# Pooling k and v of two batches with a band matrix on TensorE in place of additions on GpSimd

## The chip, the cores and the metric

The kernel runs on one core of a Trainium2 chip. A core has TensorE (PE in the profile, its weight loads PEld), VectorE (DVE), ScalarE (ACT), GpSimd (POOL) and SyncE (SP), which here issues all DMAs from one queue in order. Each engine works off its own list of instructions in order and waits on semaphores for the others. The metric is the device time of one execution in microseconds; lower is better.

## The reference

Three parts follow each other. Attention with pooled keys and values, for 4 batches, 8 heads, 576 tokens and a head size of 64; a first expert layer of 512 to 2048 to 512 with h * cos(h); and eight gated experts of 512 to 1024 to 512, whose gates are normalised over rows and columns eight times. The part that the change touches:

```python
    pool = 8
    Sp = S // pool                                          # 72 pooled rows
    k_p = k.reshape(B, H, Sp, pool, D).mean(axis=3)
    v_p = v.reshape(B, H, Sp, pool, D).mean(axis=3)
    scores = scale * np.matmul(q, k_p.transpose(0, 1, 3, 2))
    scores = scores - np.max(scores, axis=-1, keepdims=True)
    attn = np.exp(scores)
    attn = attn / (np.sum(attn, axis=-1, keepdims=True) + 1e-09)
    return np.matmul(attn, v_p).astype(np.float32)
```

The weights of the first expert layer come as float64 and are turned into float32 in the kernel. Products of the expert layers are made of three products of rounded parts (a high part and a remainder on each side).

## The kernel before

**Tiles and stages.** The 2304 tokens are 6 blocks of 384, each of three chunks of 128. A batch has 576 tokens, so block 0 needs batch one alone, block 1 batches one and two, block 2 batch two, block 3 batch three, block 4 batches three and four, block 5 batch four. The stages overlap. In the head, attention of block 0 is computed and the first unit of the expert weights is converted; then the loop over tasks (unit u of weights and block j) runs hidden products, the nonlinearity and output products, and between them takes attention of later blocks from one list (`attn_queue`) and conversions of later weights from another (`conv_queue`). The gated experts follow from about 400 us on.

**Attention.** `attn_weights` asks for the pooled keys of the batches of its block, calls `load_k` for those not there yet, loads q, makes the scores (`scores`, L277, tile psc; a product of a q chunk with `kbd`, the pooled keys of a pair of heads on a diagonal of blocks), subtracts the maximum on VectorE (L334, L335), takes the exponential on ScalarE (L336) and normalises (`normalize`: sum at L338, multiplication at L297). `attn_values` calls `load_v` where needed, transposes the probabilities on TensorE (L353, tile ptr) and multiplies them by the pooled v (L360, tile px); ScalarE and VectorE split the result into two parts (L367, L368).

**Pooling.** Batch one has its own functions. Its k is added up on VectorE and its v by TensorE: v lies in rows of tokens, 128 tokens to a tile, and is multiplied by `band`, a matrix of ones and zeros of 136 columns, of which the 72 columns from an offset select, for a tile of tokens, the pooled row that each token belongs to (`pool_first_v`, L248, five products of 512 columns). For batches two to four `load_k` and `load_v` fetch four tiles each, one per pair of heads, already laid out with the 8 members of a pool as the middle dimension (tiles kr, vr), and `pool_sum` (L200, L202) adds them in three steps of halves on GpSimd; then `fill_kbd` copies the pooled keys into one of two `kbd` tiles on ScalarE (L207). The tiles kr and vr come from the pool of buffers `rawp`, which has three buffers of one tag. The same three serve the units of weights that `load_unit` reads back (L102).

**Conversions.** `convert` turns a piece of float64 weights into float32 with one operation on ScalarE (L116), five on VectorE (L117 to L125) and one on GpSimd (L126), and writes it to memory (L127). `split` makes the two parts of weights: ScalarE the high one (L94), VectorE or GpSimd the remainder (L95).

**What sets the order.** The code records operations in program order, and a scheduler puts each engine's list in an order of its own, by dependences and by its model of times. So a change of one operation moves others on all engines.

Of the kernel before, what the change touches and what calls it, by code (L numbers as in the profile page):

```python
# [10 lines left out]
F32 = mybir.dt.float32  # L11
# [7 lines left out]
B, H, S, D = 4, 8, 576, 64  # L19
POOL = 8  # L20
SP = S // POOL
HP = H // 2
P = 128
T = B * S
DM = H * D
# [12 lines left out]
SINKHORN_ITERS = 8  # L38
EPS = 1e-9
G2 = 32  # L40
BAND0 = S // POOL // 16 * 16


# [12 lines left out]


@with_exitstack
def fused_kernel(ctx: ExitStack, tc: tile.TileContext, qT, kT, vT, v0, wa1, wb1, wa2, wb2, wg, out):
    nc = tc.nc  # L60

    const = ctx.enter_context(tc.tile_pool(name="const", bufs=1))
# [2 lines left out]
    rawp = ctx.enter_context(tc.tile_pool(name="rawp", bufs=3))  # L65
# [4 lines left out]
    ps_a = ctx.enter_context(tc.tile_pool(name="ps_a", bufs=2, space=bass.MemoryType.PSUM))  # L70
# [97 lines left out]
    def right(stack, name, bufs, **more):  # L168
        return stack.enter_context(tc.tile_pool(name=name, bufs=bufs, side="right", **more))
# [3 lines left out]
    kp = right(early, "kp", 2)  # L173
# [22 lines left out]
    def pool_sum(out, r, engine):  # L196

        n = POOL // 2
        while n > 1:
            engine.tensor_tensor(out=r[:, :n], in0=r[:, :n], in1=r[:, n:2 * n], op=ALU.add)  # L200
            n //= 2
        engine.tensor_tensor(out=out, in0=r[:, 0], in1=r[:, 1], op=ALU.add)  # L202

    def fill_kbd(b, ks):
        kbd = kbds[b % 2]
        for j in range(2):
            nc.scalar.activation(out=kbd[j * D:(j + 1) * D, :, j * SP:(j + 1) * SP],  # L207
                                 in_=ks[j * D:(j + 1) * D], func=AF.Copy)
        kpool[b] = kbd
# [11 lines left out]
    def load_first_v():  # L221

        tiles = []
        for tag in ("xl2", "xh3", "xl5"):
            t = xp.tile([P, 2, DM], F32, tag=tag, name="v0")
            for i in range(2):
                o = len(tiles) * P
                rows = min(P, S - o)
                if rows > 0:
                    nc.sync.dma_start(out=t[:rows, i, :], in_=v0[o:o + rows, :])  # L230
                    tiles.append((t[:rows, i, :], rows))
        return tiles

# [6 lines left out]
                                     in_=ks[j * D:(j + 1) * D], func=AF.Copy)  # L240
        kpool[0] = kbds[0]

    def pool_first_v(tiles):

        pv = ps_a.tile([SP, DM], F32, tag="pa", name="pv")
        for c, (t, rows) in enumerate(tiles):
            o = BAND0 - c * P // POOL
            nc.tensor.matmul(out=pv, lhsT=band[:rows, o:o + SP], rhs=t, start=(c == 0), stop=(c == len(tiles) - 1))  # L248
        vs = kp.tile([SP, H, D], F32, tag="vs", name="vs")
        nc.scalar.activation(out=vs.rearrange("p h d -> p (h d)"), in_=pv, func=AF.Copy)  # L250
        vpool[0] = vs

    def load_k(b):
        ks = kp.tile([P, HP, SP], F32, tag="ks", name="ks", bufs=1)
        for hp in range(HP):
            kr = rawp.tile([P, POOL, SP], F32, tag="raw", name="kr")
            nc.sync.dma_start(out=kr, in_=kT[:, b, hp])
            pool_sum(ks[:, hp], kr, nc.gpsimd)
        fill_kbd(b, ks)

    def load_v(b):
        vs = kp.tile([SP, H, D], F32, tag="vs", name="vs")
        for hp in range(HP):
            vr = rawp.tile([SP, POOL, 2 * D], F32, tag="raw", name="vr")
            nc.sync.dma_start(out=vr, in_=vT[:, b - 1, hp])
            pool_sum(vs[:, 2 * hp:2 * hp + 2, :].rearrange("p h d -> p (h d)"), vr, nc.gpsimd)
        vpool[b] = vs

# [38 lines left out]
    def attn_first(qcs, g):  # L307

        at = at_tile(0, g)
        for i in range(TPB):  # L310
            ps = scores(i, g, qcs[i][:, 2 * g:2 * g + 2], (ps_s, "ps") if i % 2 == 0 else (ps_a, "pa"))
            mx = sp.tile([P, 4, 1], F32, tag="mx", name="mx")
            nc.vector.tensor_reduce(out=mx.rearrange("p h o -> p (h o)"), in_=ps, op=ALU.max, axis=AX.X,
                                    negate=True)
            nc.vector.tensor_scalar(out=mx, in0=mx, scalar1=SCALE, scalar2=None, op0=ALU.mult)
            sm = sp.tile([P, 4, 1], F32, tag="sm0", name="sm0")
            for h in range(4):
                nc.scalar.activation(out=at[:, i, h, :], in_=ps[:, h, :], func=AF.Exp, scale=SCALE,
                                     bias=mx[:, h, :], accum_out=sm[:, h, :])
            normalize(at[:, i], sm)  # L320
# [140 lines left out]
    for what in 'kqfqqvfff':  # L461
        if what == "k":
            kr0 = load_first_k()
        if what == "q":
            qcs.append(load_q(len(qcs)))
        if what == "v":
            vr0 = load_first_v()
        if what == "f":
            raws.append(load_piece(0, len(raws)))
    pool_first_k(kr0)  # L470
    vpool[0] = None
    for g in range(2):
        attn_first(qcs, g)
        if g == 0:
            pool_first_v(vr0)
    for g in range(2):
        attn_values(0, g)

# [2 lines left out]
    def open_gate():  # L481
# [13 lines left out]
        nc.scalar.activation(out=wg2[:, :, :E], in_=wgr, func=AF.Copy)  # L495
        nc.vector.tensor_tensor(out=wg2[:, :, G2:G2 + E], in0=wgr, in1=wg2[:, :, :E].bitcast(F32), op=ALU.subtract)
        sel = gc.tile([G2 + E, E], F32, name="sel")
        nc.vector.tensor_tensor(out=sel, in0=ident[:G2 + E, :E], in1=ident[:G2 + E, G2:G2 + E], op=ALU.add)
        gate.update(ones=ones, wg2=wg2, sel=sel, lg=gc.tile([P, NT, E], F32, name="lg"),
                    pr=gc.tile([P, NT, E], F32, name="pr"))  # L500

    def logits(j):
# [389 lines left out]
```

## Time and profile before

| | us |
|---|---|
| median of 3 runs | 2053.98 (2053.37 to 2056.27) |
| the profiled execution, its own time | 2056.55 |
| span of its instructions | 2054.7 |
| PE busy in the span | 2008.2 (98%) |
| DVE busy | 1254.5 (61%) |
| ACT busy | 899.3 (44%) |
| POOL busy | 818.1 (40%) |

The slices of the page show where the engines are busy. The first slices are the head:

```profile
PE   6799999999999999999999999999999999999999
DVE  8987785655685555555666555555565655555553
ACT  6675566656533334333444343343343343333431
POOL 7755653433333234243443342342353432433420
PEclk8899999999999999999999999999999999999999
```

A slice is 51 us long, and a digit is the busy share in tenths (9 is 90% or more). Busy time of PE is modelled and holds overlaps; the granted clock stands as a share of 2.4 GHz, so 0.75 in a stretch is half of it at 2.4 and half at 1.2 GHz. An operation's time on DVE or POOL holds what it waits for inside the engine once it has begun.

### The profile page before, as it was taken

To read this page: it belongs to the slowest core of one execution; us is meant where nothing else is said; L and a number is where in the kernel's file an instruction comes from. 1 tells how busy PE (TensorE), PEld (TensorE's weight loads), DVE (VectorE), ACT (ScalarE), POOL (GpSimd) and SP (SyncE) were. 2 spreads that over 40 slices of the span, in tenths; PEclk is the share of its full clock that TensorE was granted. 3 is DMA by queue.
4 is the path that set the end of the run, shared out by engine and by line. 5 is a ranking of instruction groups with operands and counts; after the bars stand their busy time and mean duration, and the time that the engine had idled before them with its cause. 6 is when DMAs were issued, how large, how long until landed. Compare 5 with 4: busy or idle time off the path is not lost.

```text
span 2054.7 us, 27450 instructions
## 1 busy us (share of the span) xinstructions
PE 2008.2 (98%) x10339; PEld 1817.8 (88%) x10339; DVE 1254.5 (61%) x2003; ACT 899.3 (44%) x1781; POOL 818.1 (40%) x646
## 2 busy tenths in 40 slices
PE   6799999999999999999999999999999999999999
PEld 5689899999888889989888888888898888898887
DVE  8987785655685555555666555555565655555553
ACT  6675566656533334333444343343343343333431
POOL 7755653433333234243443342342353432433420
PEclk8899999999999999999999999999999999999999
DMA  7433331211311212212232122121132221221210
GB/s 257 140 126 124 110 121 47 83 52 62 123 63 62 68 56 82 62 62 74 70 123 72 52 83 72 52 82 62 62 107 92 69 72 54 80 72 52 83 42 31
DMA packets 53636, 167.46 MB, mean 81 GB/s; under 512 B 6112, under 2 KB 9952, under 8 KB 53504
## 3 DMA queue, kind: packets, MB, share of 16 engines
q1 hardware_dynamic: 53504, 165.72, 24.9%
q8 instruction: 81, 1.33, 0.3%
q14 instruction: 51, 0.42, 0.1%
HBM read 149.44 MB, written 16.25 MB: 81 GB/s over the span
## 4 chain that ended last, share of the span: by engine, by line
PE 88%; DVE 5%; DMA 1%; ACT 1%; issue 1%; POOL 1%; SPq 0%; DVEq 0%; ACTq 0%; POOLq 0%
PE po L135 15%; PE po L136 15%; PE po L137 15%; PE py L683 14%; PE pv L683 10%; PE px L683 10%; PE ph L136 2%; PE ph L135 2%; PE ph L137 2%; DVE m L121 1%; DVE at L297 1%; DVE cw L125 0%; DMA wb1f<-cw 0%; DVE m L119 0%; DVE r L387 0%
## 5 line engine op out<-in xcount | busy, mean ns | idle before, releaser
L95 POOL TENSOR_TENSOR wlo<-raw,whi 128x512 fp32r<-128x512 f32 x248 | 345.2, 1410 | 680.9 <-ACT gh L671 489.6
L135 PE MATMUL po<-whi,gh 128*128 128x512 f32 x1152 | 455.1, 395 | 0.6 <-DVE acc L733 0.6
L136 PE MATMUL po<-wlo,gh 128*128 128x512 f32 x1152 | 454.4, 394 | 0.0
L137 PE MATMUL po<-whi,gl 128*128 128x512 f32 x1152 | 454.0, 394 | 0.0
L94 ACT ACTIVATE whi<-raw 128x512 fp32r<-128x512 f32 x488 | 290.3, 625 | 220.6 <-PE py L683 184.8
L739 DVE SCALAR_TENSOR_TENSOR acc<-po,pr,acc 128x512 f32<-128x512 f32 x252 | 188.7, 749 | 292.4 <-PE po L137 288.2
L683 PE MATMUL py<-xc,whi 128*128 128x384 f32 x1152 | 293.7, 335 | 0.0
L95 DVE TENSOR_TENSOR wlo<-raw,whi 128x512 fp32r<-128x512 f32 x240 | 216.7, 903 | 125.6 <-ACT whi L94 60.5
L137 PEld LDWEIGHTS po<-whi,gl 128*128 128x128 f32 x1152 | 216.2, 188 | 50.1
L135 PEld LDWEIGHTS po<-whi,gh 128*128 128x128 f32 x1152 | 216.1, 188 | 42.3 <-DVE acc L733 0.8
L136 PEld LDWEIGHTS po<-wlo,gh 128*128 128x128 f32 x1152 | 215.7, 187 | 37.9
L683 PEld LDWEIGHTS py<-xc,whi 128*128 128x128 f32 x1152 | 210.1, 188 | 12.3
L683 PE MATMUL py<-xc,wlo 128*128 128x384 f32 x576 | 192.7, 335 | 0.0
L587 POOL TENSOR_TENSOR s<-raw 128x512 f32<-128x512 f32 x48 | 63.2, 1317 | 312.1 <-DMA raw<-wa 288.9
L683 PE MATMUL pv<-xc,whi 128*128 128x384 f32 x640 | 169.4, 338 | 2.0 <-DVE gl L672 2.0
L671 ACT ACTIVATE gh<-c 128x384 fp32r<-128x384 f32 x96 | 50.2, 523 | 224.2 <-DVE c L711 224.2
L135 PE MATMUL ph<-xh,whi 128*128 128x384 f32 x384 | 130.3, 343 | 5.1 <-DVE r L387 5.0
L683 PE MATMUL px<-xc,whi 128*128 128x384 f32 x512 | 134.8, 335 | 0.0
L136 PE MATMUL ph<-xl,whi 128*128 128x384 f32 x384 | 130.6, 341 | 0.7 <-DVE xl L368 0.7
L136 PE MATMUL po<-gl,whi 128*128 128x384 f32 x384 | 129.2, 337 | 0.6 <-POOL gl L390 0.6
L137 PE MATMUL ph<-xh,wlo 128*128 128x384 f32 x384 | 129.2, 337 | 0.0
L137 PE MATMUL po<-gh,wlo 128*128 128x384 f32 x384 | 128.3, 337 | 0.0
(161 smaller groups left out, 3635.9 us busy)
## 6 DMA issues: line engine op xcount, KB each, us to landing
raw<-wa SPq DMA_DIRECT2D x112, 512.0 KB, 4.5
raw<-wb SPq DMA_DIRECT2D x112, 512.0 KB, 3.6
raw<-wa1f SPq DMA_DIRECT2D x14, 512.0 KB, 3.7
raw<-wb1f SPq DMA_DIRECT2D x14, 512.0 KB, 3.7
out<-acc SPq DMA_DIRECT2D x18, 256.0 KB, 4.3
wa1f<-cw SPq DMA_DIRECT2D x16, 256.0 KB, 2.9
wb1f<-cw SPq DMA_DIRECT2D x16, 256.0 KB, 2.8
qc<-qt SPq DMA_DIRECT2D x30, 128.0 KB, 4.2
```

The lines of the kernel that those rows point to most:

```text
L94: nc.scalar.activation(out=hi, in_=src, func=AF.Copy)
L95: lo_engine.tensor_tensor(out=lo, in0=src, in1=hi.bitcast(F32), op=ALU.subtract)
L121: v.scalar_tensor_tensor(out=m, in0=high, scalar=-2**30, in1=m, op0=ALU.bitwise_and, op1=ALU.bitwise_or)
L135: nc.tensor.matmul(out=ps, lhsT=lh, rhs=rh, start=(i == 0), stop=False)
L136: nc.tensor.matmul(out=ps, lhsT=lh, rhs=rl, start=False, stop=False)
L137: nc.tensor.matmul(out=ps, lhsT=ll, rhs=rh, start=False, stop=(i == n - 1))
L297: engine.tensor_tensor(out=at[:, r], in0=at[:, r], in1=rs[:, r].to_broadcast([P, 4, SP]), op=ALU.mult)
L587: nc.gpsimd.tensor_tensor(out=out, in0=x, in1=y, op=op)
L671: nc.scalar.activation(out=gh, in_=c, func=AF.Relu)
L683: marks["pe"] = nc.tensor.matmul(out=ps, lhsT=l[:, k], rhs=r[:, c, :], start=(start and c + n == 0), stop=(last and n == 2), skip_group_ch ...
L739: nc.vector.scalar_tensor_tensor(out=a, in0=po, scalar=pe, in1=a, op0=ALU.mult, op1=ALU.add)
```

## The change

For batches two and three (`BANDED`) k and v come as rows of tokens, 128 to a tile, and are pooled by products with `band` on TensorE. `load_rows` fetches a batch's 576 rows in five DMAs into three tiles of `rawp`. `load_k` makes twenty products, four pairs of heads by five tiles of tokens, with the rows as weights and 72 columns of `band` moving, into one PSUM tile (pk) of the pool `ps_a`, from which `fill_kbd` copies. `load_v` does for these batches what was done for batch one alone: five products of 512 columns with `band` as weights, and a copy by ScalarE. Batch one's k is still added up on VectorE, and batch four's k and v on GpSimd. The host lays the tensors out to suit.

```diff
+BANDED = range(1, B - 1)
...
-    def pool_first_v(tiles):
+    def pool_v(b, tiles):
...
         pv = ps_a.tile([SP, DM], F32, tag="pa", name="pv")
         for c, (t, rows) in enumerate(tiles):
             o = BAND0 - c * P // POOL
             nc.tensor.matmul(out=pv, lhsT=band[:rows, o:o + SP], rhs=t, start=(c == 0), stop=(c == len(tiles) - 1))
         vs = kp.tile([SP, H, D], F32, tag="vs", name="vs")
         nc.scalar.activation(out=vs.rearrange("p h d -> p (h d)"), in_=pv, func=AF.Copy)
-        vpool[0] = vs
+        vpool[b] = vs
+
+    def load_rows(src):
+
+        tiles = []
+        for i in range(0, S, 2 * P):
+            raw = rawp.tile([P, 2, DM], F32, tag="raw", name="rows")
+            for c in range(2):
+                o = i + c * P
+                rows = min(P, S - o)
+                if rows > 0:
+                    nc.sync.dma_start(out=raw[:rows, c, :], in_=src[o:o + rows, :])
+                    tiles.append((raw[:rows, c, :], rows))
+        return tiles
 
     def load_k(b):
-        ks = kp.tile([P, HP, SP], F32, tag="ks", name="ks", bufs=1)
-        for hp in range(HP):
-            kr = rawp.tile([P, POOL, SP], F32, tag="raw", name="kr")
-            nc.sync.dma_start(out=kr, in_=kT[:, b, hp])
-            pool_sum(ks[:, hp], kr, nc.gpsimd)
+        if b in BANDED:
+
+            tiles = load_rows(kn[b - 1])
+            ks = ps_a.tile([P, HP, SP], F32, tag="pa", name="pk")
+            for hp in range(HP):
+                for c, (t, rows) in enumerate(tiles):
+                    o = BAND0 - c * P // POOL
+                    nc.tensor.matmul(out=ks[:, hp, :], lhsT=t[:, hp * P:(hp + 1) * P], rhs=band[:rows, o:o + SP],
+                                     start=(c == 0), stop=(c == len(tiles) - 1))
+        else:
+            ...
         fill_kbd(b, ks)
 
     def load_v(b):
+        if b in BANDED:
+            pool_v(b, load_rows(vn[b]))
+            return
```

The scheduler's lists change with it. Lines of the changed kernel stand 2 lower in its first part and 28 lower from the scores on (L305 is the old L277, L381 the old L353, L388 the old L360).

On PE, at the first block's values and the first hidden products (kbd_126 holds the keys of batch one, kbd_128 those of batch two, ph is a hidden product, px a product with v), the list before reads:

```order
L353 MATMUL ptr<-ident,at 72x128 x4
L137 MATMUL ph<-xh_278,wlo 128x384
L135 MATMUL ph<-xh_278,whi 128x384
L136 MATMUL ph<-xl_279,whi 128x384
L137 MATMUL ph<-xh_278,wlo 128x384
L360 MATMUL px<-pt,vs 64x384 x4
L277 MATMUL psc<-kbd_128,qc 64x144
L277 MATMUL psc<-kbd_126,qc 64x144
L277 MATMUL psc<-kbd_128,qc 64x144
L277 MATMUL psc<-kbd_128,qc 128x144 x2
L135 MATMUL ph<-xh_278,whi 128x384 x2
```

The list after, from the same values on:

```order
L388 MATMUL px<-pt,vs 64x384 x4
L137 MATMUL ph<-xh_278,whi 128x384 x2
L276 MATMUL pk<-band,rows 128x72 x20
L138 MATMUL ph<-xl_279,whi 128x384
L139 MATMUL ph<-xh_278,wlo 128x384
```

And, ten hidden products behind pk:

```order
L305 MATMUL psc<-kbd_128,qc 64x144
L305 MATMUL psc<-kbd_126,qc 64x144
L305 MATMUL psc<-kbd_128,qc 64x144
L305 MATMUL psc<-kbd_128,qc 128x144 x2
L250 MATMUL pv<-rows,band 72x512 x5
L305 MATMUL psc<-kbd_126,qc 128x144 x2
```

The twenty products of pk stand two hidden products behind px, where the scores with batch two's keys stood; twelve hidden products are now ahead of those scores, and the five products of pv of batch two stand between them and the next block's first scores.

On POOL, behind the first block's normalisation (cw and wlo are a conversion and a remainder of weights), the list before reads:

```order
L202 TENSOR_TENSOR ks<-kr 128x72
L200 TENSOR_TENSOR vr<-vr 72x512
L126 TENSOR_TENSOR cw<-m,cw 128x512
L200 TENSOR_TENSOR vr<-vr 72x512
L126 TENSOR_TENSOR cw<-m,cw 128x512
L200 TENSOR_TENSOR vr<-vr 72x256
L200 TENSOR_TENSOR vr<-vr 72x512
L95 TENSOR_TENSOR wlo<-cw,whi 128x512
L200 TENSOR_TENSOR vr<-vr 72x256
L202 TENSOR_TENSOR vs<-vr 72x128
```

The list after, at the same two conversions:

```order
L97 TENSOR_TENSOR wlo<-cw,whi 128x512
L128 TENSOR_TENSOR cw<-m,cw 128x512 x2
L97 TENSOR_TENSOR wlo<-cw,whi 128x512 x2
L128 TENSOR_TENSOR cw<-m,cw 128x512
L97 TENSOR_TENSOR wlo<-cw,whi 128x512
L128 TENSOR_TENSOR cw<-m,cw 128x512
L418 TENSOR_TENSOR gl<-r,gh 128x384
```

The additions of kr, ks, vr and vs are gone from between them; conversions and remainders follow one another.

On SP, at v of batch three and k of batch four (qc is q, raw_1631 and the like float64 weights), the list before reads:

```order
L265 DMA vr<-vt 72x1024
L331 DMA qc<-qt 128x256
L434 DMA raw_1417<-wb 128x1024
L331 DMA qc<-qt 128x256
L127 DMA wa1f<-cw 128x512
L257 DMA kr<-kt 128x576 x2
L434 DMA raw_1452<-wb 128x1024
L257 DMA kr<-kt 128x576
L331 DMA qc<-qt 128x256
L127 DMA wa1f<-cw 128x512
L257 DMA kr<-kt 128x576
```

The list after:

```order
L264 DMA rows<-vn 128x512
L129 DMA wa1f<-cw 128x512
L264 DMA rows<-vn 128x512 x3
L264 DMA rows<-vn 64x512
L359 DMA qc<-qt 128x256 x2
L462 DMA raw_1631<-wb 128x1024
L129 DMA wa1f<-cw 128x512
L359 DMA qc<-qt 128x256 x2
L282 DMA kr<-kt 128x576 x3
L359 DMA qc<-qt 128x256
L282 DMA kr<-kt 128x576
```

The last four DMAs of vr became five of rows; the first three of kr now follow one another, and the weights and the write that stood among them stand ahead of them or behind. On PE the scores that need these keys (kbd_128 again) stand, behind the five products of pv of batch three, after 33 hidden and output products, seven score products and twelve transposes.

## Rows read from the trace of the kernel before

**Rows 1.** Busy time by stage: window, length, engines busy (instructions), clock, DMA.
```profile
20.00:46.00 26.00, 18.20 (x92) 12.93 (x93) 24.50 (x43) 17.18 (x40) 23.59 (x27) 0.77 0.67 212
46.00:98.00 52.00, 40.59 (x220) 33.45 (x220) 51.36 (x81) 31.05 (x54) 41.70 (x44) 0.85 0.54 161
98.00:140.00 42.00, 40.17 (x242) 34.72 (x242) 38.09 (x78) 29.62 (x52) 21.16 (x22) 1.00 0.41 127
...
240.00:280.00 40.00, 34.30 (x201) 31.80 (x200) 35.07 (x57) 21.74 (x45) 26.54 (x25) 1.00 0.43 134
```

**Rows 2.** Waits of PE, 20 to 98 us: total us, times, longest.
```profile
PE psc L277 <- DVE at L335: 5.9, 2, 5.7
```

**Rows 3.** DVE groups by shape, 20 to 98 us: busy us, mean ns, idle before.
```profile
L297 DVE TENSOR_TENSOR at<-at,rs 128x288 f32<-128x288 f32 x12 | 14.0, 1220 | 0.0
L121 DVE SCALAR_TENSOR_TENSOR m<-raw,m 128x512 int32<-128x512 int32 x9 | 9.2, 1031 | 0.0
L119 DVE TENSOR_SCALAR m<-m 128x512 int32<-128x512 int32 x8 | 7.2, 910 | 0.0
...
L117 DVE TENSOR_SCALAR m<-m 128x512 f32<-128x512 f32 x8 | 6.8, 859 | 0.1
...
L124 DVE TENSOR_SCALAR cw<-m 128x512 int32<-128x512 int32 x8 | 5.8, 741 | 0.0
```

**Rows 4.** The same operations, whole span: duration min/median/max in ns.
```profile
L117 DVE TENSOR_SCALAR m<-m x32: 410/462/2117, 9.5 to 302.8; 128x512 f32<-128x512 f32 x32
L119 DVE TENSOR_SCALAR m<-m x32: 357/428/2321, 9.9 to 304.7; 128x512 int32<-128x512 int32 x32
L121 DVE SCALAR_TENSOR_TENSOR m<-raw,m x32: 674/694/4725, 10.4 to 306.4; 128x512 int32<-128x512 int32 x32
L124 DVE TENSOR_SCALAR cw<-m x32: 410/428/1711, 11.5 to 307.4; 128x512 int32<-128x512 int32 x32
L297 DVE TENSOR_TENSOR at<-at,rs x30: 444/458/2923, 47.7 to 316.9; 128x288 f32<-128x288 f32 x30
```

**Rows 5.** Stage 20 to 98 us: L200, then L202; DVE and POOL busy.
```profile
20.00:98.00 78.00, 0.00 (x0) 29.74 (x32) 0.82 0.59 178
...
20.00:98.00 78.00, 0.00 (x0) 9.13 (x16) 0.82 0.59 178
```

**Rows 6.** Timeline of PEld at 14 us: start, us, operation, idle before.
```profile
14.35 0.14 PEld L248 LDWEIGHTS pv<-v,band 128*72 128x72 f32 x1 [0.29 <-issue]
14.78 0.14 PEld L248 LDWEIGHTS pv<-v,band 128*72 128x72 f32 x1 [0.29 <-issue]
```

**Rows 7.** Timeline of PE at 404 us, a small product's six records.
```profile
404.54 0.83 PE L514 MATMUL pq<-sel,lt 40*128 40x8 f32 x6
405.30 0.44 PE L508 MATMUL pl<-xh,wg 128*128 128x384 f32 x1
```

**Rows 8.** Timeline of PE at 101 us, at full clock.
```profile
101.14 0.33 PE L136 MATMUL po<-gl,whi 128*128 128x384 f32 x1
101.31 0.34 PE L137 MATMUL po<-gh,wlo 128*128 128x384 f32 x1
101.49 0.65 PE L277 MATMUL psc<-kbd,qc 128*128 128x144 f32 x4
101.98 0.27 PE L353 MATMUL ptr<-ident,at 128*72 128x128 f32 x1
```

**Rows 9.** Timeline of PE at 43 us, behind the long wait.
```profile
43.69 1.30 PE L277 MATMUL psc<-kbd,qc 128*128 128x144 f32 x4 [5.67 <-DVE at L335]
```

**Rows 10.** The copy of pooled v from PSUM by ACT, batch one.
```profile
L250 ACT ACTIVATE vs<-pv x1: 593/593/593, 18.2 to 18.2; 72x512 f32<-72x512 f32 x1
```

**Rows 11.** The tiles kr: durations in ns, first and last start, DMA landing.
```profile
L200 POOL TENSOR_TENSOR kr<-kr x24: 482/794/1361, 16.3 to 113.7; 128x288 f32<-128x288 f32 x12, 128x144 f32<-128x144 f32 x12
L257 SPq DMA_DIRECT2D kr<-kt x12: 328/355/423, 10.0 to 106.6; - x12
L202 POOL TENSOR_TENSOR ks<-kr x12: 325/514/850, 22.4 to 116.1; 128x72 f32<-128x72 f32 x12
...
DMA to landing us min/median/max: 2.9/3.7/4.5
```

**Rows 12.** Timeline of SP at 92 us, the fourth batch's first k tiles.
```profile
92.54 1.98 SPq L257 DMA_DIRECT2D kr<-kt  x2
```

More of the change, by code (lines that the diff above doesn't have):

```diff
@@ L58, in fused_kernel @@
 @with_exitstack
-def fused_kernel(ctx: ExitStack, tc: tile.TileContext, qT, kT, vT, v0, wa1, wb1, wa2, wb2, wg, out):
+def fused_kernel(ctx: ExitStack, tc: tile.TileContext, qT, kT, kn, vT, vn, wa1, wb1, wa2, wb2, wg, out):
     nc = tc.nc
@@ L229, in load_first_v @@
                 if rows > 0:
-                    nc.sync.dma_start(out=t[:rows, i, :], in_=v0[o:o + rows, :])
+                    nc.sync.dma_start(out=t[:rows, i, :], in_=vn[0, o:o + rows, :])
                     tiles.append((t[:rows, i, :], rows))
@@ L250, in pool_first_v @@
         nc.scalar.activation(out=vs.rearrange("p h d -> p (h d)"), in_=pv, func=AF.Copy)
-        vpool[0] = vs
-    def load_k(b):
-        ks = kp.tile([P, HP, SP], F32, tag="ks", name="ks", bufs=1)
-        for hp in range(HP):
-            kr = rawp.tile([P, POOL, SP], F32, tag="raw", name="kr")
-            nc.sync.dma_start(out=kr, in_=kT[:, b, hp])
-            pool_sum(ks[:, hp], kr, nc.gpsimd)
+        vpool[b] = vs
[10 more added lines that the diff above has]
+        return tiles
+    def load_k(b):
+        if b in BANDED:
[7 more added lines that the diff above has]
+        else:
+            ks = kp.tile([P, HP, SP], F32, tag="ks", name="ks", bufs=1)
+            for hp in range(HP):
+                kr = rawp.tile([P, POOL, SP], F32, tag="raw", name="kr")
+                nc.sync.dma_start(out=kr, in_=kT[:, 1, hp])
+                pool_sum(ks[:, hp], kr, nc.gpsimd)
         fill_kbd(b, ks)
     def load_v(b):
+        if b in BANDED:
+            pool_v(b, load_rows(vn[b]))
+            return
         vs = kp.tile([SP, H, D], F32, tag="vs", name="vs")
@@ L264, in load_v @@
             vr = rawp.tile([SP, POOL, 2 * D], F32, tag="raw", name="vr")
-            nc.sync.dma_start(out=vr, in_=vT[:, b - 1, hp])
+            nc.sync.dma_start(out=vr, in_=vT[:, hp])
             pool_sum(vs[:, 2 * hp:2 * hp + 2, :].rearrange("p h d -> p (h d)"), vr, nc.gpsimd)
@@ L474, in fused_kernel @@
         if g == 0:
-            pool_first_v(vr0)
+            pool_v(0, vr0)
     for g in range(2):
@@ L854, with rows @@
     qt = q.reshape(B, HP, 2, S, D).transpose(2, 4, 1, 0, 3).reshape(P, HP, NT, P).transpose(0, 2, 1, 3)
-    kt = k.reshape(B, HP, 2, SP, POOL, D).transpose(2, 5, 0, 1, 4, 3).reshape(P, B, HP, POOL, SP)
-    vt = v[1:].reshape(B - 1, HP, 2, SP, POOL, D).transpose(3, 0, 1, 4, 2, 5).reshape(SP, B - 1, HP, POOL, 2 * D)
-    v0 = v[0].transpose(1, 0, 2).reshape(S, DM)
+    def rows(a):
+        return a.transpose(0, 2, 1, 3).reshape(-1, S, DM)
+    kt = k[::B - 1].reshape(2, HP, 2, SP, POOL, D).transpose(2, 5, 0, 1, 4, 3).reshape(P, 2, HP, POOL, SP)
+    kn = rows(k[1:B - 1])
+    vt = v[B - 1].reshape(HP, 2, SP, POOL, D).transpose(2, 0, 3, 1, 4).reshape(SP, HP, POOL, 2 * D)
+    vn = rows(v[:B - 1])
     def units_a(w):
@@ L879 @@
     arrays = {
-        "qt": c(qt), "kt": c(kt), "vt": c(vt), "v0": c(v0), "wa1": wa1, "wb1": wb1, "wa2": c(wa2), "wb2": c(wb2),
+        "qt": c(qt), "kt": c(kt), "kn": c(kn), "vt": c(vt), "vn": c(vn), "wa1": wa1, "wb1": wb1, "wa2": c(wa2), "wb2": c(wb2),
         "wg": c(wg),
```

## The prediction

> **What bounds the kernel now.** I read the view by stages first, then what TensorE waited for, then the costs of VectorE's operations, and last the rows of the operations that change. The profiled execution took 2056.55 us around a span of 2054.7 us; the median of the runs shown is 2053.98 us. The sum below is a difference within the profiled span, and I add it to the median, since nothing that lies around the span is changed.
>
> From 140 us on TensorE is almost never idle; it is idle in the head of the program, while attention, the pooling and the float64 conversions are done. Between 20 and 98 us VectorE is busy 75.9 of 78 us, GpSimd 65.3, TensorE 58.8 [rows 1]. So VectorE bounds this stage, and TensorE has 7.8 + 11.4 = 19.2 us of idle time in it, of which one wait of 5.7 us is for a subtraction in VectorE's queue [rows 1, 2]. From 98 to 140 us TensorE is busy 40.2 of 42 us: there it is the bound, with 1.8 us idle [rows 1].
>
> VectorE's 75.9 us are not all work. Its operations that read only SBUF take far longer in this stage than their usual time: the multiplication at L297 1220 ns against a median of 458, L121 1031 against 694, L119 910 against 428, L117 859 against 462, L124 741 against 428 [rows 3, 4]. Twelve, nine, eight, eight and eight of them make 9.1 + 3.0 + 3.9 + 3.2 + 2.5 = 21.7 us of excess. GpSimd is busy 84% of that time [rows 1], and I read the excess as waits for it.
>
> **What is removed.** The additions of batches two and three on GpSimd. In 20 to 98 us the pooling additions are 29.7 + 9.1 = 38.9 us of GpSimd [rows 5], 60% of its 65.3 us (two of the fourth batch's additions are among them, and the first of batch two lies ahead). If the excess falls with that share, VectorE gets back 0.6 x 21.7 = 12.9 us. Bounds: nothing, if GpSimd's remaining conversions and splits, packed closer, collide as often; 21.7 us if nothing collides any more. I take 12.9, the share that the rows give.
>
> **What is added on TensorE.** A pooled v is five products of 512 columns. The one in the trace (batch one, L248) is ten records, each starting 0.43 us after the other at full clock: 4.3 us a batch [rows 6]. A pooled k is twenty products of 72 columns, forty records, each with a 128-column load of rows as weights. No row shows that. Lower bound: by columns, half of a score record of 144 columns ((101.98 - 101.49)/4 = 0.12 us), 0.06 x 40 = 2.4 us [rows 8]. The nearest row is the product with a 128-column load and only 8 columns moving: six take 405.30 - 404.54 = 0.76 us, 0.127 each, 5.1 us for forty [rows 7]; I take it. At half clock, where four score records take 1.30 us instead of 0.65, k is 10.2 and v 8.6 us [rows 8, 9]. So the change puts 2 x (5.1 + 4.3) = 18.8 us on TensorE at full clock.
>
> **What is moved.** In the order of the change, k of batch two stands between the first hidden products, and its v right behind the first scores, about where the 5.7 us wait was. k of batch three comes among the hidden products of the second block, by my count of the products ahead of it in the last few us of that stage. So 5.1 + 4.3 + 5.1 = 14.5 us fall into the stage of 20 to 98 us. v of batch three comes behind it, where TensorE has no room: its 4.3 us are on the path whole.
>
> **The sum.** TensorE's 19.2 us of idle time take up the 14.5 us; 4.7 are left. The granted clock was 0.77 and 0.85 in the two parts [rows 1], so 2 x (0.23 x 26 + 0.15 x 52) = 27.6 us ran at 1.2 GHz, 8.4 more than the idle time; with products in the gaps these would run at 2.4 GHz, which gives 4.2 us. The stage can so shrink by 4.7 + 4.2 = 8.9 us before TensorE is its bound, and VectorE allows 12.9. Behind it comes v of batch three, +4.3. Last, k of batch four. It is still added up on GpSimd, its tiles use the three buffers that v of batch three now holds until TensorE has read them, and its scores stand behind 33 products of 384 columns, seven score products and twelve transposes: 33 x 0.17 + 14 x 0.12, with the transposes at no more than 0.12 each, is 8.8 us [rows 8]. Meanwhile a DMA must be issued and land (0.4 + 3.7), be added up (2 x 0.79 + 0.51 = 2.1), a fourth one go the same way in its buffer (6.2), and ScalarE copy twice (0.6 each, the PSUM copy's row): 13.6 us, less the 2.6 us by which the first buffer comes free ahead of the last product; 11.0 [rows 10, 11]. TensorE waits 2.2 us; the spare 4.0 us of VectorE's relief may take the stage's own 1.8 us of idle time back, so +0.4. The sum: -8.9 + 4.3 + 0.4 = -4.2 us, or 2049.8 us.
>
> Edits at nothing: ScalarE gains two copies of 0.6 us [rows 10] in stages where it is busy 17.2 of 26 and 31.1 of 52 us [rows 1]; if it were the bound, 1.2 us. SyncE issues four more DMAs (five instead of four per tensor), about 0.36 us each [rows 11]; TensorE has what is queued before them to do, and without that cover 1.4 us are late. The rows must have landed before TensorE's queue reaches them, else all behind them waits: for k of batch two they are asked for at the place where the old tiles were, at some 10 us, and land before 20; v of batch two waits for k's buffers and for a converted block's write, which costs nothing if both are done 4 us earlier, and up to 4.5 us, one landing, if not [rows 11]. v of batch four stays with GpSimd; TensorE's 5.7 us of idle time between 240 and 280 us [rows 1] stay, give or take as much.
>
> **A rule that gives another sum.** By matmul time TensorE was busy 58.8 of those 78 us, by weight loads 12.9 + 33.5 = 46.4 [rows 1]. The Trainium skill (Perfetto Trace Analysis, Identifying the Most-Contended Engine) says that matmul busy time misjudges how near TensorE is to its limit, and that the share of weight loads is to be taken. By it 31.6 us were free, 17.1 after the 14.5, more than VectorE's relief; by the rows of matmul time 4.7. That is the first rival.
>
> **Rivals.** VectorE stays the bound, TensorE taking in all that is added: -12.9 + 4.3 + 0.4 = -8.2, 2045.8 us. For it: the weight loads' 59% of the stage, and the 5.7 us wait ends on VectorE [rows 2]. Against it: TensorE's queue is in order, and what waits for a softmax can't be filled at will. This is the case of the page named above.
>
> TensorE becomes the bound and its clock gains nothing: -4.7 + 4.3 + 0.4 = 0.0, 2054.0 us. For it: after the waits that remain, as for the probabilities at L297, the clock can fall as before.
>
> k of batch four is late (the slower side). Its tiles need buffers that TensorE frees, then DMA, GpSimd, ScalarE, and TensorE's in-order queue stands at its scores meanwhile. Before, the chain from the first of its DMAs (92.54 us) to the last sum (116.1 + 0.3) was 23.9 us long [rows 11, 12]. If it is as long again, TensorE waits 23.9 - 8.8 = 15.1 us instead of 2.2: 12.9 more, -4.2 + 12.9 = +8.7, 2062.7 us. It makes the change a loss from a chain of 11.0 + 4.2 = 15.2 us on. Against it: part of the 23.9 was GpSimd's work on v of batch three, which is gone.
>
> **Chances.** The forecast 0.38, VectorE stays the bound 0.22, no gain from the clock 0.19, k of batch four late 0.21. About 0.2% (4.1 us) is what a measurement of this kernel tells from no change. The forecast lies on that edge, between -8 and -1 us by its unknown terms (k's products between 2.4 and 10.2 us, relief between 0 and 21.7): 0.21 of its 0.38 I count as faster, 0.15 as the same, 0.02 as slower. The first rival is faster, the second mostly the same (0.15; 0.03 faster, 0.01 slower), the third slower but for 0.02. Faster 0.46, same 0.32, slower 0.22. The range takes in the first rival with some 5 us below it and the third up to its middle: 2041 to 2062 us; the forecast's own is 2046 to 2053.
>
> **What would show it.** Right: L297 at 600 to 800 ns and L119 under 650 in the head; the 5.7 us wait gone; GpSimd's busy time in the first 98 us down by about 38 us; k's records at 0.11 to 0.13 us; TensorE idle under 10 us between 20 us and v of batch three. Wrong: VectorE's operations as long as before (then the excess was not GpSimd's additions); a TensorE wait of more than 4 us at the rows or at batch four's scores; records of k longer than 0.2 us at full clock.

## The result, and the profile after

The changed kernel takes 2070.11 us (median of five runs, 2064.98 to 2071.85) against 2053.98: ratio 1.0069, 95% interval 1.0058 to 1.0080. The two medians lie 16.1 us apart, and the ratio stands for 14; the kernel before, run again beside the experiments, had medians of 2055.2 to 2056.6 us, so about 14 us slower is what I go by. 4 us faster was forecast, and 2062 was the end of the range. The profiled run is the shortest of the five: 2064.98 us, span 2063.3, which is 8.6 us over the span before; its mean granted clock is 0.993, the others' 0.990 to 0.991. A clock lower by 0.0025 over 2063 us is 5.2 us of TensorE time, so what the trace lacks against the median is in size what the clock takes.

Busy time by stage after, the columns as in [rows 1]:

```profile
20.00:46.00 26.00, 23.57 (x122) 15.67 (x122) 22.02 (x41) 16.87 (x37) 13.73 (x12) 0.93 0.71 234
46.00:98.00 52.00, 44.55 (x251) 37.98 (x250) 41.44 (x87) 32.64 (x55) 15.71 (x14) 0.84 0.36 118
98.00:140.00 42.00, 41.56 (x241) 33.53 (x240) 27.56 (x60) 24.98 (x45) 15.32 (x20) 1.00 0.49 148
...
240.00:280.00 40.00, 35.46 (x205) 33.44 (x203) 34.09 (x54) 23.46 (x46) 26.68 (x26) 1.00 0.44 131
```

From 20 to 98 us GpSimd's busy time fell from 65.3 to 29.4 us and VectorE's from 75.9 to 63.5. VectorE's groups in that stretch, beside [rows 3] (L325 is the old L297; L123, L121, L119 and L126 are the old L121, L119, L117 and L124):

```profile
L123 DVE SCALAR_TENSOR_TENSOR m<-raw,m 128x512 int32<-128x512 int32 x9 | 7.1, 788 | 0.1
L325 DVE TENSOR_TENSOR at<-at,rs 128x288 f32<-128x288 f32 x12 | 6.2, 567 | 0.0
...
L119 DVE TENSOR_SCALAR m<-m 128x512 f32<-128x512 f32 x9 | 5.2, 586 | 2.2 <-ACT m L118 2.2
L126 DVE TENSOR_SCALAR cw<-m 128x512 int32<-128x512 int32 x10 | 4.8, 479 | 0.0
L121 DVE TENSOR_SCALAR m<-m 128x512 int32<-128x512 int32 x9 | 4.7, 527 | 0.1
```

The multiplication went from 1220 to 567 ns, the other four from 741 to 1031 down to 479 to 788. So the relief came: VectorE's busy time fell by 12.4 us where 12.9 was forecast, and the excess of the five groups over the medians of [rows 4] fell from 21.7 to 4.7 us. The products also took about what was forecast (the timeline of PE, start, us, operation):

```profile
31.38 5.71 PE L276 MATMUL pk<-band,rows 128*128 128x72 f32 x40 [0.48 <-DVE xl L396]
...
95.83 5.61 PE L276 MATMUL pk<-band,rows 128*128 128x72 f32 x40
```

```profile
115.91 4.60 PE L250 MATMUL pv<-rows,band 128*72 128x512 f32 x10
```

That is 11.3 us for both k and 9.2 for both v, 20.5 in place of 18.8. Next, what TensorE waited for. Before, from 20 to 140 us (engine, operation, releaser: total us, times, longest; the wait of [rows 2] leads this list too):

```profile
...
PE psc L277 <- issue: 3.7, 2, 2.2
PE ptr L353 <- DVE xl L368: 2.9, 2, 2.0
PE px L360 <- ACT pt L354: 2.6, 3, 1.2
```

After, the same stretch:

```profile
PE px L388 <- ACT pt L382: 8.3, 5, 3.8
PE ptr L381 <- issue: 0.8, 1, 0.8
PE psc L305 <- ACT at L346: 0.6, 1, 0.6
```

The wait of 5.7 us for VectorE is gone, and the wait of px for ScalarE's copy of the transposes (pt) has grown from 2.6 to 8.3 us. ScalarE's timeline shows why the longest, 3.80 us up to 87.06, lasted so long:

```profile
83.36 0.91 ACT L364 ACTIVATE at<-at 128x864 f32<-128x864 f32 x1
84.30 1.28 ACT L414 ACT_TABLE_LOAD   x1
85.59 0.52 ACT L414 ACTIVATE r<-r 128x384 f32<-128x384 f32 x1
86.02 0.51 ACT L413 ACTIVATE r<-r 128x384 f32<-128x384 f32 x1
86.43 0.57 ACT L382 ACTIVATE pt<-ptr 72x512 f32<-72x512 f32 x1
```

The copy that TensorE needs stands behind an exponential, a table load and two steps of the nonlinearity in ScalarE's own list. ScalarE was busy 49.5 of the 78 us; it is no bound by its share, but what stands ahead of one copy decides. And one wait of this size is new behind the head (PE's timeline, then stages, at 167 us):

```profile
167.06 0.69 PE L137 MATMUL ph<-xh,whi 128*128 128x384 f32 x1 [5.33 <-DVE r L415]
```

```profile
160.00:164.00 4.00, 1.73 (x14) 1.04 (x12) 4.00 (x8) 4.00 (x10) 1.31 (x1) 0.93 0.00 0
164.00:168.00 4.00, 0.94 (x3) 0.94 (x4) 3.90 (x7) 1.48 (x5) 2.96 (x3) 0.50 0.18 29
168.00:172.00 4.00, 4.00 (x19) 4.00 (x18) 1.07 (x2) 1.71 (x4) 3.56 (x4) 0.72 0.64 234
```

TensorE stood while VectorE did the steps of two conversions one after the other (158.3 to 166.1 us), and its clock was at 1.2 GHz in and behind the wait.

**An account.** TensorE's time is products at full clock, plus idle time, plus what half clock takes. From the stages of the whole head (20 to 140 us: 120 less PE's busy time; 120 x (1 - clock)) and of 140 to 400 us:

```profile
20.00:140.00 120.00, 109.68 (x610) 87.19 (x611) 91.02 (x187) 74.49 (x136) 44.76 (x44) 0.91 0.48 154
```

Against before (98.96 busy, 0.89) this is: products +20.5, idle -10.7, clock -2.4, idle from 140 to 400 us +3.0 (8.0 to 11.0). The sum is +10.4; the spans differ by +8.6. It leaves out the clock behind 140 us: from 160 to 175 us the clock is 0.77 after and 1.00 before (3.4 us lost), from 540 to 565 us it is 0.93 after and 0.80 before (3.2 us gained); here the two nearly cancel. The same account is used below for every kernel, from one profiled run each. Two kernels below have the head of the kernel before unchanged, and for them it gives 21.9 and 21.1 us of idle time from 20 to 140 us (21.0 before) and 7.2 and 7.4 from 140 to 400 us (8.0 before), so differences of 1 us in it mean nothing.

### The profile page after: what moved, and what is told of

Its sections match the earlier page's. It is cut to its first block, busy times and chain, and to the rows that moved or that the text cites. A ratio compares the mean times of both kernels' runs of the same rounds, so it can differ in the third digit from the quotient of the medians.

```text
span 2063.3 us, 27618 instructions
## 1 busy us (share of the span) xinstructions
PE 2024.0 (98%) x10439; PEld 1827.5 (89%) x10439; DVE 1241.9 (60%) x2003; ACT 900.7 (44%) x1783; POOL 778.7 (38%) x598
## 4 chain that ended last, share of the span: by engine, by line
PE 90%; DVE 3%; ACT 2%; DMA 2%; POOL 1%; issue 1%; SPq 0%; DVEq 0%; POOLq 0%; ACTq 0%
PE po L137 16%; PE po L138 15%; PE po L139 15%; PE py L711 14%; PE px L711 10%; PE pv L711 10%; PE ph L137 2%; PE ph L138 2%; PE ph L139 2%; PE px L388 1%; PE pk L276 1%; PE psc L305 1%; DVE cw L127 0%; DMA vr<-vt 0%; PE pl L536 0%
## 5 line engine op out<-in xcount | busy, mean ns | idle before, releaser
L97 DVE TENSOR_TENSOR wlo<-raw,whi 128x512 fp32r<-128x512 f32 x240 | 221.2, 922 | 124.3 <-ACT whi L96 59.6
L711 PEld LDWEIGHTS py<-xc,whi 128*128 128x128 f32 x1152 | 210.1, 188 | 12.4 <-issue 0.2
```

Source lines behind the costliest of these rows:

```text
L97: lo_engine.tensor_tensor(out=lo, in0=src, in1=hi.bitcast(F32), op=ALU.subtract)
L711: marks["pe"] = nc.tensor.matmul(out=ps, lhsT=l[:, k], rhs=r[:, c, :], start=(start and c + n == 0), stop=(last and n == 2), skip_group_ch ...
```

## The experiments

The kernel before, run beside each group, had medians from 2055.2 to 2056.6 us. Theory A: the products come on TensorE's path at their full time, and the relief on VectorE gives back about 11 us. The rivals: B, in the first four texts: the products fit into the idle time, and the loss is a new order of the scheduler with a late wait in it; O, in the later texts: the new order is the loss, whatever work was added. "Idle" and "clock" are us lost as in the account above, before's being 21.0, 8.0 and 13.2; "products" are estimates from the record times above (for float32r from 0.233 us a record). The last two columns are differences from before, the account's sum and the profiled span.

| kernel | ratio, 95% interval | products | idle 20-140 | idle 140-400 | clock 20-140 | account | span |
|---|---|---|---|---|---|---|---|
| no products | 0.9945 (0.9931-0.9959) | 0 | 16.8 | 5.1 | 10.8 | -9.5 | -11.9 |
| products added, additions kept | 1.0073 (1.0060-1.0085) | 22.7 | 19.0 | 7.3 | 12.0 | +18.8 | +15.3 |
| batch two alone | 1.0071 (1.0059-1.0084) | 10.3 | 19.1 | 9.5 | 19.2 | +15.9 | +13.8 |
| batch three alone | 1.0087 (1.0073-1.0101) | 10.3 | 17.1 | 12.7 | 15.6 | +13.5 | +17.4 |
| before, order turned | 1.0006 (0.9997-1.0015) | 0 | 24.1 | 7.0 | 13.2 | +2.1 | +2.5 |
| v alone | 1.0027 (1.0018-1.0036) | 9.2 | 19.3 | 8.1 | 4.8 | -0.8 | +1.6 |
| k alone | 1.0074 (1.0060-1.0088) | 11.3 | 18.5 | 9.2 | 16.8 | +13.6 | +18.9 |
| products doubled | 1.0176 (1.0161-1.0191) | 41 | 6.2 | 11.2 | 21.6 | +37.8 | +37.8 |
| changed, order turned | 1.0065 (1.0051-1.0079) | 20.5 | 10.9 | 10.5 | 12.0 | +11.7 | +12.1 |
| wide products | 1.0037 (1.0026-1.0049) | 19.2 | 12.6 | 12.0 | 4.8 | +6.4 | +8.8 |
| wide, rows by GpSimd | 1.0091 (1.0077-1.0105) | 19.2 | 16.6 | 11.1 | 8.4 | +13.1 | +18.0 |
| cheap products | 1.0055 (1.0041-1.0069) | 5.6 | 19.9 | 5.3 | 16.8 | +5.4 | +7.1 |
| cheap but for k of batch two | 1.0022 (1.0011-1.0032) | 9.0 | 13.4 | 10.3 | 7.2 | -2.3 | +1.9 |

The account comes within 5.3 us of the span everywhere. In k alone and batch three alone the rest may lie in the clock behind 140 us (their granted clock from 140 to 400 us is 0.98 and 0.97; the changed kernel turned round has 0.98 too, and no rest); in the two kernels with GpSimd's early DMAs it lies ahead of 20 us, where TensorE is busy 7.5 and 9.5 us instead of 11.7.

**The two halves of the change.** First the changed kernel without its products, then the kernel before with as many products that nobody reads (shown for k; for v twenty of 128 columns with the band as weights; they take 22.7 us where the change's take 20.5):

```diff
-            ks = ps_a.tile([P, HP, SP], F32, tag="pa", name="pk")
...
+            ks = tiles[0][0][:, :HP * SP].rearrange("p (h s) -> p h s", s=SP)
...
-            pool_v(b, load_rows(vn[b]))
+            tiles = load_rows(vn[b])
+            vs = kp.tile([SP, H, D], F32, tag="vs", name="vs")
+            nc.scalar.activation(out=vs.rearrange("p h d -> p (h d)"), in_=tiles[0][0][:SP], func=AF.Copy)
```

> The change without its pooling products: rows of k and v of batches two and three are loaded as in the change, and the tiles are filled from the first tile of rows by ScalarE, so the pooled sums of these two batches are left out. Theory A (TensorE pays the products' 20 us, and the relief of VectorE gives back about 10): 2040 to 2047 us, under the kernel before. Theory B (the products fit into idle time, the loss is a new order of the scheduler): within 6 us of the change, 2060 to 2072.

```diff
+        if b in (1, 2):
+            pk = ps_a.tile([P, HP, SP], F32, tag="pa", name="pk")
+            for hp in range(HP):
+                for c in range(5):
...
+                    nc.tensor.matmul(out=pk[:, hp, :], lhsT=ident[:rows, :], rhs=band[:rows, o:o + SP],
+                                     start=(c == 0), stop=(c == 4))
```

> The kernel before with all its additions on GpSimd, and products of the same count and streamed columns beside them, on data that is already there, whose results nobody reads. Theory A: of about 20 us the idle time before 98 us hides about half, 2060 to 2068. Theory B: hidden, 2052 to 2058.

Measured 2044.72 and 2071.05 us. The relief by itself is worth 11 us, and the products by themselves cost 15. The second is more than A expected and far over B. TensorE idles 19.0 us from 20 to 140 us although 22.7 us of products stand in its list, by the same view where the changed kernel idles 10.3:

```profile
20.00:140.00 120.00, 101.00 (x612) 83.30 (x610) 103.73 (x176) 68.62 (x131) 81.61 (x89) 0.90 0.48 155
```

So the idle time took up little of the products: of 21.0 us it gave 2.0, and of the 8.0 behind 140 us 0.7. (22.7 us of products cost 15.0 by the medians; of the 7.7 between, 2.7 are idle time and 1.2 the clock, and the rest is not placed.) With the additions gone it is the same. The stages of the kernel without products, 20 to 140 and 140 to 400 us:

```profile
20.00:140.00 120.00, 103.19 (x593) 86.24 (x592) 107.55 (x208) 81.93 (x157) 55.55 (x50) 0.91 0.53 169
140.00:400.00 260.00, 254.86 (x1480) 245.45 (x1480) 189.84 (x328) 160.04 (x322) 138.42 (x116) 0.99 0.29 97
```

And the changed kernel's second stage (its first stands with the account):

```profile
140.00:400.00 260.00, 248.96 (x1449) 238.79 (x1448) 189.58 (x330) 158.15 (x316) 137.40 (x117) 0.99 0.29 94
```

From 20 to 400 us TensorE idles 21.9 us without the products and 21.3 with them; before it was 29.0. So the relief shortened the idle time, by 7.1 us, and the products hardly did.

The two halves do not add up: 11 us less and 15 more make 4, and the change costs 14. With the additions gone the products cost 25.4 us by the medians (20.5 by the profiled spans), and with the products there the relief is worth 1. These runs do not show why.

**One batch at a time** (`BANDED` as (1,), then as (2,), which index batches two and three; the host then lays out all of k and v both ways):

> Batch two alone by products, batches three and four on GpSimd. Theory A: 10 us of products, at a place where TensorE had 5.7 us of wait and a low clock, against half of the relief: 2050 to 2058. Theory B: whatever the order gives; if it holds the late wait of 5 us behind 155 us, 2060 or more.

> Batch three alone by products. Theory A: 10 us of products where TensorE is nearly full, little relief: 2057 to 2066, slower than batch two alone. Theory B: no difference between the two that the waits behind 140 us don't explain.

Measured 2070.78 and 2073.77: each half of the change costs as much as the whole. A fails here: half of +14 is 7, and both lie over its ranges. A late wait is not the reason either: batch two alone has no wait of TensorE over 1.5 us from 140 to 400 us. With half the relief the idle time falls by 2 to 4 us alone, and the clock loses more, 19.2 and 15.6 us instead of 13.2. For batch two the extra lies behind the products, from 98 to 140 us, where before is at full clock with 1.8 us idle [rows 1]:

```profile
98.00:140.00 42.00, 35.06 (x185) 28.70 (x186) 32.51 (x65) 27.60 (x49) 13.78 (x14) 0.88 0.32 102
```

**How much is order.** Lists rearranged with no work changed: before with `for hp in reversed(range(HP))` in the loop of load_v, which moves more rows of TensorE's list than the change does, and the changed kernel with the same edit, where it touches batch four alone.

> The kernel before, with one loop turned round: load_v fetches and adds the four pairs of heads in the order 3, 2, 1, 0. No instruction is added or removed, but the scheduler's lists come out quite different (on TensorE more rows move against the kernel before than the change itself moves). Theory A (the products' price: they cost what they take on TensorE, and the relief on VectorE gives about 11 us back): no product is added and no addition goes, so 2051 to 2060 us, as the kernel before. Theory O (the order: a rearranged list makes new waits, each followed by half clock, and that is most of what the change cost): more than 6 us away from 2056, to either side, with waits of TensorE over 2 us at places where the kernel before has none.

> The changed kernel with the four pairs of heads of batch four's v fetched and added in the order 3, 2, 1, 0: the same instructions, a somewhat other list. Theory A (price of the products less relief): 2070 as the changed kernel, 2065 to 2074, even if the wait of 5.3 us at 162 us goes or another comes. Theory O (order): more than 5 us off 2070.

Measured 2057.35 (1.1 us over before) and 2068.59 (1.5 us below the changed kernel). The wait of 5.3 us stays in the second. So a new order need not cost anything: these two moved the time by 1 to 2 us. That another order costs more is not excluded by them.

**v alone, k alone, twice the products.** `BANDED` for v only, for k only; and each product made twice (`enumerate(tiles * 2)`).

> The change for v alone: v of batches two and three by products, k of both still added up on GpSimd. Theory A: 2 x 4.6 = 9.2 us of products; of the relief of 11 us (what the kernel without products gained) the share of v's additions, some 60 per cent, is 6.6; so 2056 + 2.6 = 2059 us, 2055 to 2063. Theory O: not told by the products; as the halves by batch came out at 2071 and 2074, 2064 to 2076 is as likely as anything.

> The change for k alone: k of batches two and three by products, v of both still added up on GpSimd. Theory A: 2 x 5.7 = 11.4 us of products less some 4.4 us of relief: 2056 + 7 = 2063 us, 2059 to 2067. Theory O: anything from 2050 to 2076; together with the kernel for v alone the two changes against before would not add up to the +14 of the whole.

> The change with each of its products made twice (the second pass starts the sum again, so the result is the same): 20 us more on TensorE where the change has its 20. Theory A: the idle time of TensorE does not take them up, so 2070 + 20 = 2090 us, 2084 to 2096. Theory of the forecast (idle time takes up products as long as there is some; TensorE still idles about 12 us from 20 to 98 us in the changed kernel): 2074 to 2082. Theory O: within 10 us of 2090, as the lists move again.

Measured 2061.39, 2072.00 and 2092.99. v and the doubled products come out as A expects; k alone is 9 us dearer. Its timeline shows one reason, the first k at almost twice its time; the doubled one shows it larger:

```profile
33.82 10.04 PE L277 MATMUL pk<-band,rows 128*128 128x72 f32 x40 [0.48 <-DVE xl L397]
```

```profile
32.08 18.60 PE L278 MATMUL pk<-band,rows 128*128 128x72 f32 x80 [0.48 <-DVE xl L398]
```

```profile
32.00:36.00 4.00, 3.92 (x23) 3.52 (x24) 3.19 (x5) 2.38 (x4) 3.31 (x3) 0.78 0.82 243
36.00:48.00 12.00, 12.00 (x49) 10.75 (x48) 6.21 (x9) 1.26 (x2) 6.79 (x6) 0.50 0.46 159
```

TensorE was busy without a gap, and from 36 us on its clock stayed at 1.2 GHz. Both runs of k came right behind waits of px and pk, of 0.68 and 0.48 us. That alone is not the cause: in the changed kernel k of batch two comes behind waits of the same length and takes 5.71 us, with the clock at 1.00 from 32 to 36 us; there it falls behind k (0.64 from 36 to 40 us).

**Do narrow products make the clock fall?** Blocks of products that nobody reads, put where TensorE never waits: first of 20, 40 and 100 narrow ones with one set of weights and of 5, 13 and 32 wide ones, then 20 to 200 narrow ones, each with another load (the loop of the second):

```diff
+        for n in range(nk):
+            nc.tensor.matmul(out=t[:, :72], lhsT=w.bitcast(F32)[:, n % 4 * P:(n % 4 + 1) * P], rhs=ident[:, :72], start=True, stop=True)
```

> The kernel before, with products that nobody reads put into six steps of the gated experts, where TensorE never waits and its clock is full: 20, 40 and 100 products of the shape of the pooled k (128-column load, 72 columns moving, two records each), and 5, 13 and 32 of the shape of the pooled v (72-column load, 512 columns moving). By the records of the changed kernel (0.140 and 0.43 us) they take 5.6, 11.2, 28 and 4.3, 11.2, 27.5 us, 88 in all. Theory N (the clock in the head falls only because of waits): every block at full clock, 2056 + 88 = 2144 us, 2138 to 2150. Theory H (the products of k let the clock fall while they run without a gap, as the doubled ones seem to have done): the block of 100 runs at half clock for most of its length, 45 to 56 us long instead of 28, that of 40 perhaps, the three of v at full clock throughout; 2160 to 2185 us.

> The kernel before, with blocks of 20, 40, 100, 20 and 200 products that nobody reads put into five steps of the gated experts, of the pooled k's shape and now each with a load of other weights, as the pooled k has. At 0.140 us a record (two a product) they take 5.6, 11.2, 28, 5.6 and 56 us, 106 in all. Theory N (narrow products with loads keep the clock): every block at full clock, 2056 + 106 = 2162 us, 2155 to 2170. Theory H (they let it fall while they run without a gap): the blocks of 100 and 200 at half clock for most of their length, 2200 to 2250 us; the blocks of 20 at full clock or with half clock at their end.

Measured 2134.75 and 2138.69 us, below both theories' numbers, because a record took 0.112 us here and not 0.140 (320 x 0.112 + 100 x 0.43 = 79 us, measured 78; 760 x 0.112 = 85, measured 83.5). In the second, the block of 40 in PE's timeline, and a stretch inside the block of 200 by stage:

```profile
913.05 9.04 PE L695 MATMUL pt<-ident,whi 128*128 128x72 f32 x80
```

```profile
1326.00:1368.00 42.00, 42.00 (x378) 42.00 (x378) 0.00 (x0) 0.00 (x0) 1.56 (x2) 1.00 0.04 14
```

The clock is 1.00 through 42 us of them. H falls as put: where TensorE does not wait, narrow products that begin at full clock keep it. In the head it is not settled. In the doubled kernel k began at 32.08 us and the clock fell inside it (0.78 from 32 to 36 us, then 0.50), and once it had fallen the narrow products ran at 1.2 GHz for as long as they lasted, as they did in k alone. Why it fell inside them there and not in the changed kernel, and why it did not rise under them (their columns, their data, other waits close by), these runs do not show. Where TensorE never waits, a product costs its whole time.

**Cheaper products.** k by five products of 512 columns and four transposes; the same with rows by GpSimd's DMAs; the same in float32r; and that with batch two's k back in float32 from SyncE.

```diff
+            pn = ps_a.tile([SP, DM], F32, tag="pa", name="pn")
+            for c, (t, rows) in enumerate(tiles):
+                o = BAND0 - c * P // POOL
+                nc.tensor.matmul(out=pn, lhsT=band[:rows, o:o + SP], rhs=t, start=(c == 0), stop=(c == len(tiles) - 1))
...
+            nc.scalar.activation(out=kt_s, in_=pn, func=AF.Copy)
             ks = ps_a.tile([P, HP, SP], F32, tag="pa", name="pk")
             for hp in range(HP):
+                nc.tensor.transpose(ks[:, hp, :], kt_s[:, hp * P:(hp + 1) * P], ident[:SP, :SP])
```

> The changed kernel with k pooled as v is: five products of 512 columns with the band as weights, a copy by ScalarE, and four transposes of 72 rows, in place of the twenty products of 72 columns. A batch of k then takes 4.6 + 4 x 0.12 = 5.1 us of TensorE instead of 5.7, and no long run of narrow products. Theory H (narrow products let the clock fall): 1.2 us less by the records and 2 to 6 less by the clock, 2062 to 2068 us, and no half clock in the 3.4 us behind k. Theory N: 2069, 2065 to 2073.

> The kernel with wide products for k and v (the one that ran at 2064 us), its rows fetched by DMAs that GpSimd issues instead of SyncE, all in float32: products at 18 us, as there, and DMAs and lists nearly as in the kernel with cheap products (2067 us). Theory A with DMAs (products cost their time, the DMAs from GpSimd cost what is missing): 2067 + 12.4 = 2079 us, 2074 to 2084, 15 above the same products with SyncE's DMAs. Theory O (whatever has products loses by its order, not by their time): 2062 to 2072, as the cheap ones.

> The pooling by wide products (five of 512 columns for k and for v, transposes for k), with rows and band as float32r, which drops the low bits of k and v of batches two and three, so that a product takes one pass; the rows are fetched by DMAs that GpSimd issues. A record of 512 columns of that type takes 0.233 us in the experts, so a batch's k is 1.2 + 0.45 and its v 1.2 us: 5.6 us for both batches in place of 20. Theory A (price of the products less relief): 2056 + 5.6 - 11 = 2051 us, 2046 to 2056, faster than both kernels. A rival: issuing twenty DMAs occupies GpSimd and VectorE's relief is lost, 2057 to 2063. Theory O (loss by the order, or rows that come late): 2062 to 2075 as all kernels with products so far.

> The kernel with cheap products, but k of batch two as wide float32 products from rows that SyncE fetches, so that GpSimd issues no DMA in the first 20 us; k of batch three and both v in float32r as before (low bits of these dropped). Products: 5.1 + 1.65 + 2.4 = 9.2 us. Theory A with DMAs: 2056 + 9.2 - 11 = 2054 us, up to 2061 if the later DMAs of GpSimd cost too. Theory O: 2062 to 2075.

Measured 2064.32, 2074.43, 2066.73 and 2060.33. The wide k gains 5.8 us on the changed kernel. By the account 1.3 us of it are products and 6.0 the clock (0.96 from 20 to 140 us instead of 0.91), with 3.3 us more idle time against it. Its time lies in H's range and under N's; a lower loss of clock without the narrow products is what H says for the head, but one kernel does not settle it. The cheap products alone missed A by 16 us. The second kernel tells most of it: the same rows by GpSimd cost 10 us with the products unchanged, and going from there to cheap products gives 7.7 of the 13.6 us by which these are shorter. GpSimd's timeline in the second kernel has the early DMAs, and TensorE's two waits for the first q came to 12.5 us, instead of 8.5 with rows by SyncE (8.1 before):

```profile
2.47 0.68 POOL L264 DMA_DIRECT2D rows<-kn  x1
...
3.42 2.15 POOL L264 DMA_DIRECT2D rows<-kn  x4
```

```profile
PE psc L308 <- DMA q<-qt: 12.5, 2, 8.4
```

With those five back on SyncE the kernel comes to 2060.33, at the upper end of what A expected with its DMAs (2054, up to 2061). No version with products beats the kernel before. What does (no products) leaves the sums out.

## Why the prediction was wrong

- VectorE's relief, 12.9 us: right. VectorE's busy time fell by 12.4 us from 20 to 98 us, and without the products the kernel gained 11.3. The Trainium skill (SBUF — State Buffer, Who interferes with whom) says that a VectorE operation with two SBUF inputs contends with a GpSimd instruction that reads SBUF, and one in a two-port mode with GpSimd. The trace agrees: L325 and L123 have two, and fell from 1220 to 567 and from 1031 to 788 ns while GpSimd's busy time fell [rows 3]. The three groups with one input fell as well (the old L119 from 910 to 527 ns); whether they ran in such a mode no trace here shows.
- Products at 18.8 us: 20.5. A k record took 0.140 us instead of 0.127, a v record 0.46 instead of 0.43: +1.7.
- **"TensorE's 19.2 us of idle time take up the 14.5 us; 4.7 are left", and the stage loses these too: the step that failed.** In all, the forecast needs 18.8 us less idle time (its sum of -4.2 less 18.8 of products and plus 4.2 of clock); the trace has 7.7 less. That is 11.1 us of the 12.8 between -4.2 and the +8.6 of the profiled span. The products are 1.7 and the clock 1.8 (2.4 gained, not 4.2); the three make 14.6, over by the 1.8 by which the account of the changed kernel is over. The idle time was read as room under VectorE as the bound. By the rows it is waits in chains that begin on TensorE itself (scores, transposes) and come back through VectorE or ScalarE. Products took little of it: from 20 to 400 us, 2.7 of 29.0 us with the additions kept and 0.6 of 21.9 with them gone. With the relief the waits moved from VectorE to ScalarE's list, as the px rows show; that this holds the idle time up was seen in the trace, not tried.
- The rival by weight loads, 31.6 us of headroom: 22.7 us of added products alone cost 15.3 us of span, so no such room was there. The Trainium skill (Perfetto Trace Analysis, Identifying the Most-Contended Engine) takes MFU (the share of peak arithmetic) and the share of weight loads for how near TensorE is to its limit; for what more work costs in this head, neither that share nor matmul time told it.
- The rival that went over to the slower side, k of batch four late: not so. In the changed kernel its chain from first DMA to last sum is 128.1 + 0.3 - 117.8 = 10.6 us instead of 23.9 [rows 11, 12], and no wait of scores stands behind it. The direction of that rival was right, its mechanism wrong. TensorE as the bound with no clock gain, 2054.0, was 16 us short. All three rivals let the idle time take up the 14.5 us as the forecast did. The prediction names the ground against it, that what waits for a softmax can't be filled at will, but sets it against the first rival alone and not against its own sum.

```profile
L202 POOL TENSOR_TENSOR kr<-kr x8: 487/645/803, 120.8 to 127.3; 128x288 f32<-128x288 f32 x4, 128x144 f32<-128x144 f32 x4
L282 SPq DMA_DIRECT2D kr<-kt x4: 328/328/328, 117.8 to 122.6; - x4
L204 POOL TENSOR_TENSOR ks<-kr x4: 327/332/342, 122.3 to 128.1; 128x72 f32<-128x72 f32 x4
```

- The signs: most of those for a right forecast came, and the time was wrong. The 5.7 us wait went, the old L297 came to 567 ns (600 to 800 was named) and the old L119 to 527, GpSimd's busy time in the first 98 us fell by 37.6 us, and TensorE idled 9.9 us from 20 us to v of batch three at 115.9. Only k's records missed to the dear side (0.140 us). The last sign could not tell idle time that products fill from idle time that the relief shortens.

What stays open: why half of the change costs as much as all of it, and why products and relief do not add up. The account says where (idle time and clock from 98 us on), not why the waits fall there; and the 5 us between the profiled run and the median have no trace.

## What to carry to other kernels

Do not take idle time between dependent steps for room: unless a run shows otherwise, count added work at about its full time. Here added products cost 15.0 us for 22.7, 25.4 for 20.5, 22.9 for another 20.5, and 7.7 for 13.6. Moving work to an engine that is busy 98% of the span pays only if the relief elsewhere is larger than the work; 11 us against 20 was not, and the loss was larger than their difference. To learn which half of such a change pays, run each half alone: the change without its new work, and the new work without the change.

## What was not expected of the hardware

- The narrow products took 0.112 us a record with 128 rows in all of them and 0.140 in the pooling, where the last of five tiles has 64 rows. In the changed kernel's trace records of 128 rows start 0.111 or 0.112 us apart there too, and 0.166 to 0.205 us around the records of 64 rows.
- At 1.2 GHz TensorE went through 12.00 of 12 us of narrow products with the clock at 0.50, while 42 us of them begun at full clock stayed at 1.00.
- With five DMAs issued by GpSimd at 2.5 to 5.6 us TensorE's waits for the first q came to 12.5 us; with the same rows asked for by SyncE, from 10.4 us on, to 8.5, and before to 8.1.
